# A new written-out order for all engines, and 26 small steps that change between ScalarE and VectorE

## The chip, the cores and the metric

The kernel runs on one core of a Trainium2 chip. A core has TensorE (matrix products into PSUM), VectorE and ScalarE (elementwise work; both read PSUM), GpSimd and SyncE (here almost only issuers of transfers). Each engine works through its own list of instructions in order and waits on semaphores for the others. The metric is the device time in microseconds of one execution. In the profile PE is TensorE's matmuls, PEld its weight loads, DVE VectorE, ACT ScalarE, POOL GpSimd, SP SyncE.

## What is computed

A block-sparse attention over 4 batches x 8 heads x 768 tokens x 64, followed by a gated feed-forward layer with a convolution of width 3 over the tokens:

```python
scores = scale * np.matmul(q, k.transpose(0, 1, 3, 2))
scores = np.where(mask, scores, -1000000000.0)      # window, first and last block, 3 sampled blocks a row
attn = np.exp(scores - max); attn = attn / (sum + 1e-09)
x = np.matmul(attn, v)                              # heads side by side: (4, 768, 512)
h = np.maximum(x @ w_in, 0.0)                       # 512 -> 1024
conv_out = sum of conv_w[k] * h shifted by k - 1    # along the tokens
out = (h * sigmoid(conv_out)) @ w_out               # 1024 -> 512
```

Inputs and output are float32; the kernel computes in bfloat16 with float32 sums.

## The kernel before

Heads go in pairs: `P` numbers the 16 pairs, four to a batch. For each pair, keys and queries are brought into a layout with the head's 64 columns and 24 mask rows on the partitions (tiles `e` and `o`, one of five slots), so that one product gives masked scores. For the first five pairs TensorE turns them (`k_tr`, line 470; `q_tr`, line 508) and ScalarE or VectorE copies the result (`k_cp`, `q_cp`; all copies go through `dcopy`, lines 328 for ScalarE and 330 for VectorE); for the others a transposing transfer on SyncE does (`xb`, line 585), and VectorE copies it to the slot (`stg_cp`). The mask rows are made once from small tiles (`nblk`, line 280, `a3`, `a4`, `m_q`, `m_k`) and copied to the other slots (`m_kc`, `m_kh`, `m_h1`, `m_slot`).

The attention is cut into 144 units of eight 128x128 blocks, in nine segments of tokens (two a batch, the last one split). Of each unit TensorE makes the scores in two halves (`s`, line 746, into one of two PSUM tiles `st`; the halves of unit u are s#2u and s#2u+1), ScalarE one exponential over 128x1024 (`exp`, line 757, to one of eight tiles `pt`), and TensorE the product with the values in two halves (`av`, line 779, into one of two tiles `av`). The values come by transfer and are copied by VectorE or ScalarE (`v_cp`, to `vt`). At the end of a pair VectorE divides by the sums (`rcp`, `norm`, lines 696 and 698) and the tokens are turned, by transfer (`x_xb`, line 707) or by TensorE (`x_tr`, line 717, with a copy `x_cp`).

The feed-forward part of a segment runs between the units of the next ones: `f1` (line 895) gives a feature chunk in one of two PSUM tiles `mix`; `relu` takes it out, on ScalarE (line 915) or VectorE (line 917); `mul` and `add` (lines 949, 959) are the convolution on VectorE, in the last segment `conv` (line 970) on TensorE; `tanh` (line 998 or 975) is ScalarE's; `g1`, `g2` (lines 1001, 1006) are the gate on VectorE; `f2` (line 825, at the very end line 810) is the output product, `ev` its eviction from PSUM on ScalarE or VectorE to `o2s`, and `out` the transfer to memory.

At the start TensorE runs 45 matmuls on a cleared tile (`warm`, line 1027; the tile is cleared by VectorE, `warm_mem`, line 224) and 12 more a little later (`fill`, line 1034).

The order of all this is not worked out when the program is built: the steps are collected in a graph, and `put_down` takes them in the order of a written-out text, `ORDER`. Two characters name a step; for a step that two engines can do a third names the engine (P, A, V, G, S); then come the numbers of the buffers that it takes. The order in the text is the order of each engine's list.

Of the kernel before, what the change touches and what calls it, by code (L numbers as in the profile page):

```python
# [25 lines left out]
1A0470S481O1490T4a1U44b1V4c2404d2634e271TV34f2c14g2e04h2f4i2k24j2m11aV1oV0N1pV5H65k5l5p5q5K15L5M75u5v5z5P05Q  # L26
5A05I4O15R05U15V5W15J5a05N610625O5S5T5X5Y6324PV00J5bV5B20D5C5Z35+661675D15EV6416b06c5/0651B160V0K1DV1CV6836d4
0w0v6g16hhq0hr6i56l06m6n6ht1hu6t16uhsV0hvVhO0hQhP6v7hI0hJ6y06zhw1hxhKA6A0hyVhRhS6D16E69hz0hA6F16a1P16e6f6j6I0
6k6J6ohBA1QVhW11RVhT6q0hX6r6K26Q1hF06RhGhC1hD6S3hEAhHVhU6V06W6+11W06p06/6X47056w6x6B73074hL1hM781756hNA796C6G
7a77g06H6L6M6T17h6U6Y1Z17i07l17m6Z717276777q07r7b7n1hYhZi221XV41YVi3i4h+hV06N1i5ia36O1+Vh/ib7d21/V25V4i0ic7ei6  # L30
7s27v17w7c0ii07jio17kid7D07E7x37o7p7t7u7y7z7F4i76s1280292g12h6P7f7I17J7N07G17H7O7A37K5i17P67Biei8i92aV02bVifig
ih2dV02iV17Cijip7S17Tiq7X07Lik7U77Y7M7Q7R831847Vir7Z0851880897Wil8d18e7+8a22jVisV04k2n4l2s34mimV18002lV12tV281
iu18i08j8f38k4ix0iyizV8q18riviwViS4iTiUiV8v08wiA0iBiD1iE8s58x6iCAiFAi+0iW2o22p2qV22rV2u2002v22x2w8A18B7/08F086
878GiG08b8c8g8hiJ1iH8C78H0iXiIA8l8m8t18K18L8S08T8uiK2108yj08n1i/8oj122ViLV23Vj61j28M18U28z8X18Y8D8E8I8J90091
8Z3925j38N8O08ViM1951iP0969769d08WiQiNiOA8+9e8/939i194989j998P2j7iYj8j4iZj98Qj59a3iRVja9bje29f79k1jfjgjhji9n0
9o9p3jE1jbjs09g19s19t9u69h9l9x09yjt9z79mjF9F19q9r9G9v9w9A9K09L9B0jcjdjGjujj9H19M62F2G42C2D02Q2I2H2N2O12R32T2S
2Y2Z22y08222z2J18p8R9c9P19Q9R4jkjljHjIV29C02AV39Djv9I9U09Va019Ja1jN1jOjwA39W0a22jK0jLjMA1jPV0Gk63a50a6aa1jQ19N
abjT0jRk7k8jSVk9jUa75ac3jVA2/30032312Kaf0agak1alah7jZ1j+am1j/A9O9SjW09T9X9Yas0a31ata4a8jXa9ax1ayk31k4ke4kakb0L
kg9Z10H2BVjYVkm0knkf2LV4au6az4aC0aDaE0k00adk1aH1aeaIk2AaiajanaP0aQaJ2jm0jnkh9+ki2MVap2k5Vkcku1aU1aVaR5aW3kjjo
aZ0a+jpao0avawb21b3jy1aAaBaFaGaKaLa/7aqkv2EV32PV4kpkd1kob70b8kqkxaM3kk2+V0aNkwkl9E32U22Vin330jxarit349/b46jqA4  # L40
jzbf1bgb94jAjBbk0kI0aS1blaTaXaYaObh0krbm2jCA1bp1b0bqb1b5kJbu0bvb6ksky2WV02XVktbr5kzkAkBkC1babb0kD373833a3b13f
3c3d3ebw13mbC1bDbc035V1kEkKbH0kFbE3bIbM1bNkLkGV339A1bdkMV036VkO1kPbibJ7bO6kQVbR0bSkR0kSbT4kTVla2lblcldlebW1bj
bXbnbobsbY0kX1c20c3btkU0c71c8c42c95kYkVbxbykWAkZVbz2bAli3cc0cdbF1bGch1cibKl11ce1lfbLl2cp0cj3cqk+0bPbQbUbVbZb+0
cu1ljlklll3Vlmb/1lgc0cr7lnlhloc5l71cvk/l0Alq4cz0c6cacbcfcgcAcw6l40lplrlsltl5l8ckcE1clcFcm3l9VlucB0l6Aly0lzcnlB
lAlC3p3n03q23u3r3s3tcG4cJ0cKcs1ctcxcycClM0cL2lvcR1lG1cDcScW0cT5cHcXcY3cIlNcMcN0lHcUcVc/1d0d40d5lDjDbe03g13hjJ
c1bB3v23wcokHd17lwlxd66cZlIc+lOdc1ddde43iV2lElFd2lP3jVlQV1lJdh0lKA2didj5dm1dnm20m3d3do73E3B3F43J3G3xV3m4V0cO0
cPme1mfmgV3yVdr0d7dsm50m6dw1d8dxdt1m7Vmq1mrmsmtmud913oV23H3T3U33C13Idy03Y3V3W3Q3R23X43443df1mb1dE0dFdG2m80m9mc
dJ1mdAmaAdadKdgdO0dPdL6dQ3mh1mk0mlmidkdT1dUdldpdqdudvmjAd/0e0dzmn1dV4e41e5dA0dHdImoe15e67mpAe90eaeb1mvmy2mmVmz
mG3mImHmJmKmAdB2mBdCmCmO4lS0dMdNdRee1dSefdWdXlTe21e3lY1eg0mLdY3mwmx0mPlUej0eklZl+lVe7l/mDmQdZmRmMmS3DV3mEel2
m0A3e8er1esecew0edehexet6kN3kjr3K03LlR3Z1cQ1lWA0mFn01eieB1eCemn1mN3MV4mTey3eD4mUmV3NVeo0epmW0mXen0mYmZeG0eH  # L50
m+A4n2n3db3+3/V03zlLdDn4V140V3SV4eO1eP3Pd+nf0m1423leq2lX3O3An5ngnc1nd45A0eI5eQ7neAnhVnC0eT0eUeY1eZn90nan61n7
eV1e+0nEnDnbVn8AnFnu1f10f2euevf61f7nl0ezf32nmni1fe0f86nvnGnwnHnxnnVffeAnjeEnkVfj1fkeFeJeKfg3fl4nynzeL1nK2nLeM
nMnIeR1eSeWeXfo0fpno0e/f0ft1fuf4f5fq5f9nr1nsfv7fa0fB0fCnpfhfG1fHfifmfnfrfsfwfxfb2nNnAnJnqVnBntAfcnOfy3nS3fD1
fI0fL0fMfzn+1fN2fT1fUfE1fFo40nTnUnVnWfY0fJfZfKnPfV641eNfdfAf+3nXnQfOn/o5nRg11g2fPfQ0fW0fXf/g90g0g34gao0o6gb5g4
ge1gffRnYnZo7o1o2V2o8A3gg7gj0gkg5om0ong610MooA1gl1op1oqgc1gr1g7orVoK4oMoLoNoOov0gsgt0os1gdowoxAgw0otouAgxgB1gh
# [1014 lines left out]
```

## Time and profile before

| | |
|---|---|
| runs | 204.57, 204.63, 204.76 us; median 204.63 |
| span of the profiled execution | 202.8 us |
| time around the span (median of the runs less the span) | 1.8 us, so the profiled execution's own time is about 204.6 |
| busy, of the span | PE 97%, ACT 94%, DVE 90%, POOL 28% |
| granted TensorE clock | full in all 40 slices |

The span goes from the first to the last instruction. A busy share is the sum of an engine's instructions without overlaps; as matmuls are pipelined and their ends are modelled, PE looks fuller than it is, and the distance from the start of one matmul to the start of the next says more than its length. In a timeline a row is: start, time from the first start to the last end, engine, line, operation, output<-input, shape, count, and in brackets the idle time before it with what ended it. In the chain a row is start, length, engine, output and line.

### The profile page before, as it was taken

The page shows a single profiled execution, that of the slowest core. Times are in us where ns is not written, and L with a number is a line of the kernel's source. Part 1 is how long each engine was busy: PE and PEld are TensorE (multiplying, and loading weights), DVE is VectorE, ACT ScalarE, POOL GpSimd, SP SyncE. Part 2 cuts the span into 40 slices and gives each one's busy share as a digit, 9 for nine tenths or more (in the row PEclk, how much of TensorE's full clock was granted, in tenths as well). Part 3 has the DMA queues.
Part 4 walks back from the last instruction along what each step waited for, and adds up shares of the span by engine and source line. Part 5 has one row for each costly group of instructions (what it writes and reads, how often), then busy time and mean ns, then how long its engine had stood idle before and what let it go on. Part 6 is the DMA issues. An engine that isn't in the chain of part 4 may idle for free.

```text
span 202.8 us, 6814 instructions
## 1 busy us (share of the span) xinstructions
PE 196.8 (97%) x2708; PEld 153.9 (76%) x2708; DVE 181.8 (90%) x572; ACT 189.7 (94%) x251; POOL 57.5 (28%) x112
## 2 busy tenths in 40 slices
PE   7899999999999999999999999999999999999993
PEld 7799977986788777877688877876678877876742
DVE  7999989999999979999899988999899968999950
ACT  6999999999999999999999998999999989998842
POOL 8870568630520354202534328400000000000000
PEclk9999999999999999999999999999999999999999
DMA  6999999999998399956869699994321202001515
GB/s 143 177 223 207 182 135 132 167 171 151 155 122 129 61 141 154 213 106 132 133 108 159 82 197 218 135 176 115 124 72 24 41 14 68 13 10 60 204 63 202
DMA packets 53655, 25.96 MB, mean 128 GB/s; under 512 B 39616, under 2 KB 50584, under 8 KB 53624
## 3 DMA queue, kind: packets, MB, share of 16 engines
q0 software_dynamic: 19984, 11.24, 43.7%
q1 hardware_dynamic: 33208, 13.87, 34.6%
q8 instruction: 21, 0.34, 0.7%
q10 hardware_dynamic: 432, 0.43, 0.6%
q14 instruction: 10, 0.08, 0.1%
HBM read 23.08 MB, written 6.29 MB: 145 GB/s over the span
## 4 chain that ended last, share of the span: by engine, by line
PE 78%; ACT 15%; issue 3%; DVE 2%; DMA 1%; ACTq 0%
PE st L746 25%; PE mix L895 18%; PE mix L825 17%; PE av L779 14%; ACT pt L757 11%; DMA o2s<-in_k_dram 1%; DVE e L330 1%; ACT m L998 1%; PE mix L810 1%; PE st L825 1%; PE av L970 1%; ACT nat L328 1%; PE mix L508 1%; ACT hE L915 0%; ACT o2s L328 0%
## 5 line engine op out<-in xcount | busy, mean ns | idle before, releaser
L757 ACT ACTIVATE pt<-st 128x1024 bf16<-128x1024 f32 x144 | 140.6, 1039 | 1.8 <-PE st L746 0.9
L779 PE MATMUL av<-vt,pt 128*128 128x65 bf16 x1152 | 59.9, 193 | 0.2 <-DVE vt L330 0.2
L779 PEld LDWEIGHTS <-pt 128*128 128x128 bf16 x1152 | 52.3, 97 | 9.9 <-issue 0.3
L895 PE MATMUL mix<-xT,winb 128*128 128x384 bf16 (+2 forms) x288 | 53.6, 308 | 0.1
L949 DVE TENSOR_SCALAR m<-hE,cw 128x382 bf16<-128x382 bf16 (+2 forms) x192 | 49.3, 316 | 0.5 <-ACT hE L915 0.2
L825 PE MATMUL mix<-woutb,gT 128*128 128x512 bf16 x176 | 47.1, 379 | 0.3 <-DVE gT L1006 0.3
L746 PE MATMUL st<-o 88*128 88x128 bf16 (+1 forms) x240 | 43.9, 229 | 0.4 <-ACT pt L757 0.3
L746 PE MATMUL st<-o,e 88*128 88x128 bf16 (+1 forms) x228 | 43.4, 233 | 0.0
L746 PE MATMUL st<-e,o 88*128 88x128 bf16 (+1 forms) x224 | 42.3, 234 | 0.2 <-ACT pt L757 0.2
L746 PE MATMUL st<-e 88*128 88x128 bf16 (+1 forms) x208 | 40.9, 239 | 0.1
L746 PEld LDWEIGHTS <-o 88*128 88x128 bf16 x464 | 34.7, 97 | 7.7 <-issue 0.8
L746 PEld LDWEIGHTS <-e 88*128 88x128 bf16 x436 | 33.0, 97 | 7.1 <-issue 0.4
L959 DVE TENSOR_TENSOR m<-m 128x764 bf16<-128x764 bf16 (+2 forms) x64 | 33.5, 532 | 0.4
L895 PEld LDWEIGHTS <-winb 128*128 128x128 bf16 x288 | 24.0, 97 | 8.0 <-issue 0.5
L998 ACT ACTIVATE m<-m 128x764 bf16<-128x764 bf16 (+2 forms) x32 | 26.3, 829 | 0.5 <-DVE m L959 0.3
L825 PEld LDWEIGHTS <-gT 128*128 128x128 bf16 x184 | 15.0, 97 | 9.3 <-DVE gT L1006 0.5
L417 POOL COPY pace<-pt 1x1 bf16<-1x1 bf16 x24 | 6.2, 257 | 49.9 <-ACT pt L757 49.8
L1006 DVE TENSOR_TENSOR gT<-m,hE 128x764 bf16<-128x764 bf16 (+3 forms) x36 | 18.0, 510 | 0.5
L698 DVE TENSOR_TENSOR xtok<-av,rcp 128x384 bf16<-128x384 f32 (+2 forms) x36 | 18.2, 506 | 0.3
L915 ACT ACTIVATE hE<-mix 128x384 bf16<-128x384 f32 (+2 forms) x36 | 17.7, 507 | 0.7 <-PE mix L895 0.5
L240 POOL DMA_DIRECT2D nat<-in_q_dram x23 | 16.8, 733 | 3.2 <-issue 2.5
L917 DVE TENSOR_SCALAR hE<-mix 128x384 bf16<-128x384 f32 x28 | 15.3, 549 | 2.6 <-PE mix L895 2.2
(84 smaller groups left out, 157.4 us busy)
## 6 DMA issues: line engine op xcount, KB each, us to landing
out_dram<-o2s SPq DMA_DIRECT2D x23, 256.0 KB
vn<-in_v_dram POOLq DMA_DIRECT2D x16, 192.0 KB, 5.0
nat<-in_k_dram POOLq DMA_DIRECT2D x15, 192.0 KB, 4.7
nat<-in_q_dram POOLq DMA_DIRECT2D x7, 192.0 KB, 5.2
winb<-in_moe_w_in_dram POOLq DMA_DIRECT2D x2, 512.0 KB, 9.5
woutb<-in_moe_w_out_dram POOLq DMA_DIRECT2D x4, 256.0 KB, 8.2
nat<-in_q_dram POOLq DMA_DIRECT2D x8, 96.0 KB, 4.5
nq<-in_q_dram POOLq DMA_DIRECT2D x5, 96.0 KB, 5.2
```

Of the source, the lines that this page charges most:

```text
L240: return op(name, {eng: occ}, lambda e: on(e).dma_start(out=dst(), in_=src), prio, deps, dma=(kind, service), **kw)
L698: nm = op("norm", {"DVE": t_dps(128 * C)}, lambda e: nc.vector.tensor_tensor(out=xtok_t[xk.index][:, 0:C].rearrange("p c h d -> p h c d"), ...
L746: nc.tensor.matmul(out=st[:, 128 * x:128 * (x + n_)], lhsT=QK[kc % 2][s][0:88, 1, hh, kc // 2, :], rhs=QK[par][s][0:88, 0, hh, idx:idx + n ...
L757: nc.scalar.activation(out=pt_t[ptb.index], in_=st_t[stb.index], func=AF.Exp, bias=0.0, scale=0.125)
L779: nc.tensor.matmul(out=o[:, off:off + 65], lhsT=pt_t[ptb.index][:, 128 * x:128 * x + 128], rhs=V_t[vslot_b[P].index][:, hh, kc, 0:65], sta ...
L825: nc.tensor.matmul(out=acc(), lhsT=gT_t[gb.index][:, ffc, 128 * t:128 * t + 128], rhs=woutb[:, ffc, :], start=(ffc == 0), stop=(ffc == NFF ...
L895: nc.tensor.matmul(out=mix_t[hb.index][:, w1 * y:w1 * y + w1], lhsT=winb[:, fc, 128 * ffc:128 * ffc + 128], rhs=xT_t[xt_buf[n].index][:, f ...
L915: i = nc.scalar.activation(out=dst, in_=src, func=AF.Relu, bias=0.0, scale=0.5)
L949: i = nc.vector.tensor_scalar(out=m_t[cb.index][:, x, y, 0:w], in0=hE_t[heb.index][:, f0 + y, t0 + x:t0 + x + w], scalar1=cw[:, x, f0 + y: ...
L959: nc.vector.tensor_tensor(out=m[:, a_, :, 0:w], in0=m[:, a_, :, 0:w], in1=m[:, b_, :, 0:w], op=ALU.add)
L998: th = [op("tanh", {"ACT": t_act(2 * w) + 0.04}, lambda e, cb=cb, w=w: nc.scalar.activation(out=m_t[cb.index][:, 0, :, 0:w], in_=m_t[cb.in ...
L1006: i = nc.vector.tensor_tensor(out=gT_t[gtb.index][:, f0:f0 + 2, t0:t1], in0=m_t[cb.index][:, 0, :, 0:w], in1=hE_t[heb.index][:, f0:f0 + 2, ...
```

## The change

Only the text `ORDER` is replaced. Both texts hold the same 1,789 steps. Every buffer number stays with the step that had it, and each buffer passes from user to user in the same sequence. The lists of SyncE and GpSimd, which issue nearly all transfers, are the same; the lists of TensorE, ScalarE and VectorE are in another order. 26 steps change their engine:

- from ScalarE to VectorE (16): `m_q#1`, `m_kh#1`, `m_h1#1` (mask rows), `q_cp#3`, `v_cp#11`, `v_cp#15`, `x_cp#6`, `relu#3`, `relu#21`, `relu#42`, `ev#2`, `ev#3`, `ev#4`, `ev#12`, `ev#21`, `ev#23`;
- from VectorE to ScalarE (10): `cast_k#1`, `k_cp#2`, `relu#20`, `relu#23`, `relu#25`, `relu#38`, `relu#44`, `ev#7`, `ev#13`, `ev#14`.

(A number counts the steps of a name as the code makes them.) The text itself, cut to its first and last lines:

```diff
--- before.py
+++ after.py
@@ -18,47 +18,47 @@
 ORDER = """
-000x010z020B0407080905060b1e00a1f1c01q11s11801m11t1E21G21H030y0e0c0gV0d0nV0f0A0i0hA0WA30UA0oAr41r5r6r7r8r9rarb
-rcrdrerfrgrhrirjrkrlrmrnrorprqrrrsrtrurvrwrx0Y01210ZA014A0VA13A0mA0XV0jV0+V0lV0t0uryrzrArBrCrDrErFrGrHrIrJrK
-15017A16ArLrM4n04o0/14s14t1g11j04p00q10V0p11V1hV11lV1kV4u11dV01iV4x04yrN0rOrPrQ4C14D4z2rRrSrTrUrVrWrXrY4H04I
-4E34J44q14r4v4w4Q14R4S54A4B4F4G0s0r1rV14V04W4K1u04X64+14/5071x11vV21yV1zV4L0530544T4U4Y4Z5c15d510E15505e10C1wV
-4M01FV24N0F0k5h05i1I0525j21JV35m15n5o31L1561NV575811MV5r05s5f15g5w15x1KV1911n00I5t45y55F05G1bV591S30O0P0Q0R46
...
-qr1qsqu1qvpQqCpRq60q7qDq0pXqtAqw3qG4qxq2q3qypYpZqc1qJ1qKqdqO0qL1qeqHq4qMq5q8q9qNqIqaA3qfqPqQqRqgA4qbqhqSA0qTS
-qU0qVqWqXq+1qYA2qZSq/r0r1r2Ar3A
+040708090500060WA30b1e00C0e0a0hV0c1f1c0021q1011s1180030d0UA1m10XA0gV1t1E21G21Hr41r50oVr6r7r8r9rarb0f0A0xrc0ird
+0Brerf0lVrgrhrirjrkrlrm0jVrnrorprq0Y0rr0nVrsrtrurvrw0ZA0121rx0t0mV13A0u0/1ryrzrArB14ArCrD10A4n00VA0+V4orErFrG
+rH11VrI4p0rJ150rKrLrM4s117V16A4t4x0rN0rO4u10q4y1g1rP0z1j00p0D4C11hV11lV4z24D0y4H01kVrQrR1dV01iV4IrS0r4q14r4E3
+4J44v4Q11rV14R4w1u04V04W4A4B4S54X64FrT4+14/1S34GrU1vV2rV1x1rW0s530rX1zV5071yV544KrY4L01FV20E14T1wV5c15d4U550
+5e14Y4Z514M00O5h05i521I00F5m14N5n1L1560P0Q570G1JV31NV5j21MV5r05s0R5f15o3191465t41KV1A05w15x5g5k5y5475l5F05G1bV
...
+pjolqFqtAq60qCqu1pXpRo3pYqvqc1q2q7pZqdqG4qHqw3qJ1qKqDq3qeq4qIofq5qL1q8qMq9qfqxqyqNqO0qPqgV4qQqaA3qRqSA0q+1q/
+qU0r0r1qVqbqhqWqXqYV2r2AqTSqZSr3A
 """
```

Read out, the lists of the three engines begin so. VectorE before:

```
ident_mem#0 v_one#0 warm_mem#0 v_one#2 a_mem#0 v_one#4 pad_mem#0 v_one#1 nblk#0 ident24#0 m_q#0 a3#0 m_h1#0
a4#0 v_one#3 m_k#0 cast_k#1 m_kc#0 k_cp#1 m_kh#0 m_slot#1 k_cp#2 m_slot#0 k_cp#3 k_cp#4 q_cp#7 q_cp#6 v_cp#0
k_cp#5 m_slot#3 m_slot#2 v_cp#1 k_cp#6 q_cp#10 q_cp#11 he_zero#0 k_cp#7 rcp#0 v_cp#2 norm#0
```

VectorE after:

```
ident_mem#0 he_zero#0 nblk#0 m_q#1 ident24#0 a_mem#0 warm_mem#0 pad_mem#0 a3#0 m_q#0 m_h1#1 a4#0 v_one#3
v_one#0 m_k#0 v_one#4 m_kh#0 m_kc#0 m_h1#0 m_kh#1 k_cp#1 k_cp#3 q_cp#3 m_slot#1 v_one#2 m_slot#0 he_zero#1
k_cp#4 q_cp#7 v_one#1 q_cp#6 v_cp#0 k_cp#5 m_slot#2 v_cp#1 k_cp#6 m_slot#3 q_cp#11 q_cp#10 v_cp#2
```

ScalarE before, then after (`ld_` are transfers that it issues):

```
ld_q0#0 ld_k0#1 m_q#1 cast_k#0 cast_q#0 m_h1#1 k_cp#0 q_cp#1 cast_q#1 q_cp#0 m_kh#1 q_cp#3 q_cp#2 exp#0 exp#1
exp#2 exp#3
...
ld_q0#0 ld_k0#1 cast_k#0 cast_q#0 cast_k#1 k_cp#0 q_cp#0 q_cp#1 k_cp#2 cast_q#1 exp#0 q_cp#2 exp#1 exp#2 exp#3
exp#4 exp#5
```

TensorE before, then after:

```
warm x30 k_tr#0 q_tr#0 warm x13 q_tr#1 warm x2 s#0 s#1 k_tr#1 s#2 s#3 k_tr#2 q_tr#3 s#4 s#5 fill x4 s#6 s#7
fill x8 s#8 s#9 av#0 av#1 av#2 av#3 s#10 s#11 av#4 av#5 av#6 av#7
...
warm x23 k_tr#0 warm x6 q_tr#0 warm x1 k_tr#1 warm x6 s#0 s#1 warm x6 q_tr#1 warm x3 s#2 s#3 s#4 fill x2 s#5
k_tr#2 fill x1 q_tr#3 s#6 s#7 s#8 fill x2 s#9 fill x1 av#0 av#1 av#2 s#10 s#11 av#3 k_tr#3 s#12 s#13 av#4 av#5
av#6 fill x1 s#14 s#15 av#7
```

Further on: VectorE has `v_cp#14`, `ev#12`, `stg_cp#20` and `stg_cp#21` ahead of `norm#24` where it had them (the eviction: ScalarE) behind it, and `relu#42` follows `norm#24`; TensorE has `f1#80` and `f1#81` ahead of `f1#82`, `f1#83`, `s#238` and `s#239`, not behind them. In the last steps TensorE ends with the first column half of the last block, not the second; the evictions `ev#21` and `ev#23` are VectorE's, `ev#20`, `ev#22` and `ev#24` stay ScalarE's.

More of the change, by code (lines that the diff above doesn't have):

```diff
@@ L26 @@
[L26 to L55, printed above, removed]
```

38 lines of the change are left out of this document (34 added, 4 removed).

## The prediction

> **What bounds the kernel now.** I read the page's busy shares and its chain first, then the chain in order of time, then the PE's own timeline for the places where it really stands still.
>
> ```profile
> span 202.8 us, 6814 instructions
> PE 196.8 (97%) x2708; PEld 153.9 (76%) x2708; DVE 181.8 (90%) x572; ACT 189.7 (94%) x251; POOL 57.5 (28%) x112
> PE 78%; ACT 15%; issue 3%; DVE 2%; DMA 1%; ACTq 0%
> ```
>
> The chain of work that ended last lies on TensorE for 78% of the span. Busy shares overstate (ends of matmuls are modelled), so I look at starts in the chain:
>
> ```profile
> 39.13 0.94 ACT pt L757
> 40.11 0.87 ACT pt L757
> ...
> 84.08 0.44 PE st L746 x6
> 84.53 0.33 PE mix L895 x2
> 84.85 0.12 PE av L779 x4
> ```
>
> Around 40 us exponentials follow each other; at 84 us a piece of TensorE work starts when the one before it ends (84.08 + 0.44 = 84.52, 84.53 + 0.33 = 84.86). That holds from 67 to 189 us. So the end is set by three things: when TensorE begins real work, how much work it has (unchanged here), and where it stands still. Once the head is past, the larger standstills are these (TensorE's timeline; a row whose next row starts late hides a gap):
>
> ```profile
> 18.51 0.41 PE L779 MATMUL av<-vt,pt 128*128 128x65 bf16 x8
> 18.98 0.22 PE L746 MATMUL st<-o 88*128 88x128 bf16 x1
> ...
> 41.81 0.28 PE L779 MATMUL av<-vt,pt 128*128 128x65 bf16 x4
> 42.10 0.22 PE L746 MATMUL st<-o 88*128 88x128 bf16 x1
> ...
> 47.59 0.27 PE L746 MATMUL st<-e,o 88*128 88x256 bf16 x1
> 48.14 0.61 PE L825 MATMUL mix<-woutb,gT 128*128 128x512 bf16 x2 [0.28 <-DVE gT L1006]
> ...
> 66.43 0.28 PE L779 MATMUL av<-vt,pt 128*128 128x65 bf16 x4
> 66.99 0.22 PE L746 MATMUL st<-o 88*128 88x128 bf16 x1 [0.28 <-ACT pt L757]
> ...
> 189.01 1.58 PE L895 MATMUL mix<-xT,winb 128*128 128x128 bf16 x20
> ```
>
> Four av matmuls take 0.12 us (the 84.85 row), so the gaps are 0.47 - 0.24 = 0.23, 0.29 - 0.12 = 0.17, 0.55 - 0.11 = 0.44 and 0.56 - 0.12 = 0.44; the 20 short matmuls at 189 would take 19 x 0.056 + 0.22 = 1.28, so 0.30 is waiting. Together **1.58 us**. That is what a better order can win behind the head, and the whole size of the question.
>
> **The change, part by part.** *Buffers and transfers.* Every buffer index stays with its user, and the lists of SyncE and GpSimd are the same. Cost 0 by themselves; a transfer moves only as far as its producer does.
>
> *The head, TensorE's start.* Rows of VectorE and TensorE before:
>
> ```profile
> 0.82 0.11 DVE L223 MEMSET ident<- 128x64 uint32 x1 [0.82 <-PEq L1054]
> ...
> 0.94 0.11 DVE L224 MEMSET warm<- 128x64 uint32 x1
> ...
> 1.36 0.53 DVE L280 COPY nblk<-ident 24x768 bf16<-24x768 bf16 x1
> ...
> 1.82 0.40 DVE L267 CAST ident<-ident 24x24 f32<-24x24 bf16 x1
> 2.22 0.47 DVE L300 TENSOR_SCALAR e<-nblk 24x256 bf16<-24x256 bf16 x2
> ```
>
> ```profile
> 1.10 3.22 PE L1027 MATMUL st<-warm 128*128 128x128 bf16 x30 [1.10 <-DVE warm L224]
> 4.20 0.34 PE L470 MATMUL mix<-ident,nat 128*128 128x128 bf16 x3
> ...
> 4.79 0.90 PE L1027 MATMUL st<-warm 128*128 128x128 bf16 x13
> ```
>
> The memset of the warm-up tile was VectorE's third instruction. In the new list it stands behind nblk, which cannot start before 1.36 because it reads GpSimd's identity, one pair of mask rows (0.47, taken over from ScalarE), the small cast (0.40) and another memset (0.1). So it starts near 1.36 + 0.46 + 0.47 + 0.40 + 0.1 = 2.8 to 2.9 and the first warm-up 0.16 later (0.94 to 1.10): **3.05 instead of 1.10**. TensorE takes its list in order, and 23 warm-ups stand ahead of the first key transposes. Thirty took 4.20 - 1.10 = 3.10 us, 0.104 each while the clock is still slow (later thirteen took (0.90 - 0.22)/12 = 0.057 each), so 23 take 2.4 and the key transposes start at about **5.45 instead of 4.20**. ScalarE's share:
>
> ```profile
> 4.96 0.47 ACT L328 COPY e<-mix 64x384 bf16<-64x384 bf16 x1
> 5.45 0.26 ACT L328 COPY o<-mix 64x128 bf16<-64x128 bf16 x1
> 5.74 0.35 ACT L328 CAST nat<-o2s 128x192 bf16<-128x192 f32 x1
> 6.12 0.37 ACT L328 COPY e<-mix 64x256 bf16<-64x256 bf16 x1
> ...
> 7.58 4.66 ACT L757 ACTIVATE pt<-st 128x1024 bf16<-128x1024 f32 x5
> ```
>
> Three slow transposes need 0.5 until the last is out, so the key copy starts near 6.0 (was 4.96); with 0.47, 0.37 and 0.26 behind it the last query copy ends at 7.1, and the first scores start at 7.2; before they followed the copy that ended at 6.12 + 0.37 = 6.49. Loss there 0.7. Ahead of the first exponential ScalarE now has another key copy (taken from VectorE, costed as the 0.47 row) and the cast of head 1 (0.35): it starts near 8.0, against 7.58.
>
> *The head, VectorE.* Head 1's query transposes need that cast, so they run at 8.1. Their second copy was ScalarE's and is now VectorE's, ahead of the mask copies to slot 1; behind it VectorE's whole list waits until about 8.35.
>
> ```profile
> 7.05 0.70 DVE L330 COPY o<-o 24x1536 bf16<-24x1536 bf16 x1
> ...
> 8.15 0.76 DVE L330 COPY e<-e 24x1536 bf16<-24x1536 bf16 x1
> ...
> 9.32 0.55 DVE L330 COPY e<-mix 64x768 bf16<-64x768 bf16 x1
> ...
> 10.65 0.57 DVE L330 COPY vt<-vn 128x768 bf16<-128x768 bf16 x1
> ```
>
> ```profile
> 11.28 0.64 PE L779 MATMUL av<-vt,pt 128*128 128x65 bf16 x16 [0.21 <-DVE vt L330]
> ```
>
> 8.35 + 0.3 for the copy, + 0.72 + 0.78 for the two mask copies (starts to next starts) gives 10.15. The key copy of pair 1 (was 9.32) also waits for its transposes, which TensorE now does behind the scores of unit 2: 10.4. From there to the value copy was 10.65 - 9.32 = 1.33, and that copy takes 0.57: it ends at 12.3, and the first av, which before too waited for it, starts at **12.35 instead of 11.28**, 1.07 later. Six filler matmuls (0.057 each) and one av step (0.12), which stood ahead of unit 5's scores in the gaps, now stand behind them, where TensorE has no gap: 0.46. TensorE is then late by 1.0 to 1.5 when unit 10's scores start; **I take +1.4**. Bounds: 0.7 (only the first scores' loss, the rest absorbed) and 1.5.
>
> *The Trainium skill, beside this.* The rows show the full rate about 3 us after the first warm-up. The Trainium skill (TensorE: Matmul & The Clock Gate, Part 1) says that the clock opens after about 3.4 us of sustained activity, counted in a window that runs freely. By that the full rate would come at 6.45 or later instead of 6.0, and up to eight more warm-ups and transposes of the head would run at half rate. This is the third rival below.
>
> *The middle.* ScalarE loses the relu at 32.5 us ahead of the standstills of 41 to 67 us, and has one 0.37 copy more behind its first exponential; so its load against TensorE there is as before, and as TensorE arrives 1.4 late but ScalarE only about 1, part of the 0.23 + 0.17 + 0.44 + 0.44 goes. Bounds 0 and -1.58 (with the one at 189); **I take -0.9**. The exchanges of relus and evictions from 67 us on cost nothing while TensorE stays the later one; ScalarE's idle is their cover.
>
> *140 to 165 us, VectorE.* Rows of VectorE before:
>
> ```profile
> 143.49 0.56 DVE L698 TENSOR_TENSOR xtok<-av,rcp 128x384 bf16<-128x384 f32 x1
> ...
> 145.01 0.69 DVE L330 COPY o2s<-mix 128x512 f32<-128x512 f32 x1 [0.50 <-PE mix L825]
> 145.73 0.56 DVE L330 COPY o<-stg 64x1536 bf16<-64x1536 bf16 x1
> 146.32 0.36 DVE L330 COPY vt<-vn 128x768 bf16<-128x768 bf16 x1
> ```
>
> The normalisation at 143.49 gets two slot copies (0.56 each), a value copy (0.36) and an eviction taken from ScalarE (costed as the 0.69 row) ahead of it: 2.2 us. Behind it waits a relu taken from ScalarE, and for its bank wait feature matmuls that TensorE has moved 1.1 us closer. Bounds 0 and +2.2; I take +0.3, the size of TensorE's existing wait for VectorE (0.28 at 48.14).
>
> *The tail.* The last eviction moves to VectorE:
>
> ```profile
> 199.59 0.37 ACT L328 COPY o2s<-mix 128x256 f32<-128x256 f32 x1 [0.50 <-PE mix L810]
> ```
>
> At the ratio of the 145.01 row to the same copy on ScalarE it costs below 0.1 more; its transfer goes out through SyncE instead of ScalarE. I take 0, bounds -0.1 and +0.1.
>
> **Sum.** +1.4 - 0.9 + 0.3 = **+0.8** on a span of 202.8, so 203.6. The median of the runs, 204.63, is 1.8 above the span; the forecast is 204.63 + 0.8 = **205.4**.
>
> **Rivals.** *Faster: the standstills of 18 to 67 and 189 us all go.* TensorE arrives late, so ScalarE gets ahead and every exponential is ready. For it: ScalarE's list is the shorter one later on. Against: it must win over 1.4 + 0.4 to be told from no change, and 1.58 is all there is, unless the head loses only its lower bound. With 0.7 - 1.58 = -0.9 it gives 203.7. It decides where the head's loss stays under 1.1. *No change:* the head's loss and the gains cancel within 0.4. *VectorE becomes the bound at 140 to 165 us:* 1.4 - 0.9 + 2.2 = +2.7, 207.3. For it: VectorE is 90% busy, takes on five evictions of 512 columns and gives back three. Against: it stood idle 0.50 at 145.01. *The clock opens late:* eight instructions at 0.104 instead of 0.057 are 0.4 more in the head: 205.8.
>
> **How the numbers follow.** About 0.2% (0.4 us) is what can be told from no change. Forecast 0.45; late clock 0.07; VectorE 0.13: slower 0.65. No change 0.17. Faster 0.18. The range runs from the fast rival, 203.7, to VectorE's bound, 207.3; past each end lies less than a tenth.
>
> **What would show it.** In the changed profile: first warm-up near 3.05, first key transposes near 5.45, first exponential near 8.0, first av near 12.35 behind a wait for VectorE's vt; standstills of 41 to 67 us smaller; TensorE without gaps from 67 to 140; waits for VectorE near 146 to 165. I am wrong if the first av starts before 11.8, or if waits over 1 us appear on TensorE elsewhere.

## The result and the profile after

The changed kernel takes **215.04 us** (median of four runs, 212.10 to 216.47), the kernel before beside it on the same chip 204.60 (204.49 to 204.76). The ratio is **1.0454, 95% interval 1.0384 to 1.0524**: slower by about 9.3 us (0.0454 x 204.6). Ratios are worked out from the fast runs alone, which leaves out the one of 216.47, so they are not the quotients of the medians. The forecast was 205.4 with a range of 203.7 to 207.3: the sign was right, the size far out of the range.

The profiled run is the fastest of the four, 212.10 us with a span of 210.3. Page of the changed kernel (busy times, chain, two groups of instructions):

```profile
span 210.3 us, 6827 instructions
PE 200.1 (95%) x2708; PEld 155.3 (74%) x2708; DVE 183.3 (87%) x579; ACT 187.9 (89%) x244; POOL 59.0 (28%) x112
PE 51%; DVE 32%; DMA 8%; ACT 3%; issue 3%; POOL 0%; DVEq 0%; POOLq 0%
L757 ACT ACTIVATE pt<-st 128x1024 bf16<-128x1024 f32 x144 | 141.6, 1038 | 6.8 <-PE st L746 6.0
L895 PE MATMUL mix<-xT,winb 128*128 128x384 bf16 (+2 forms) x288 | 56.9, 312 | 3.0 <-DMA xT<-xtok 2.4
```

The chain, which lay on TensorE for 78%, lies there for 51% now; VectorE has 32% and the DMAs 8%. (VectorE's share is not all its own: at 146.43, below, the chain goes from a transpose back to a gate step of VectorE that the transpose does not read.) ScalarE's exponentials wait 6.0 us for scores, and the feature matmuls 2.4 us for a transfer, in one piece.

To see where the time goes, compare the starts of the same exponential in both traces (their order is the same). At these times of the kernel before, the changed one is late by:

| start before, us | 8 | 15 | 30 | 50 | 58 | 68 | 88 | 127 | 138 | 149 | 159 | 170 |
|---|---|---|---|---|---|---|---|---|---|---|---|---|
| late by, us | 1.0 | 1.4 | 1.7 | 1.2 | 1.5 | 2.2 | 2.7 | 2.9 | 3.2 | 7.1 | 7.4 | 6.8 |

Three parts: 1.4 us in the head, a slow growth to 3.2, and a step of 3.9 between 138 and 149 us. The last is the largest and has a plain cause. (This is the fastest of four executions; the part between 26 and 73 us is larger in the traces of runs 1 and 2 below.)

**The step at 138 to 149 us.** One step of VectorE was moved by 114 us: `m_l#0`, three small scalings that make `mlast`, the mask for the last tile (line 344). VectorE's timeline, before and after:

```profile
16.75 0.46 DVE L344 TENSOR_SCALAR mlast<-nblk 24x128 bf16<-24x128 bf16 x3
```

```profile
130.48 0.69 DVE L344 TENSOR_SCALAR mlast<-nblk 24x128 bf16<-24x128 bf16 x3
```

Its first reader is a transfer, `m_last#0` (`o<-mlast`, line 240), and that stands in the list of SyncE, which issues in order. SyncE's waits after, then its timeline before and after:

```profile
SPq L240 <- DVE mlast L344: 9.3, 1, 9.3
```

```profile
118.09 1.05 SPq L833 DMA_DIRECT2D out_dram<-o2s  x2
119.25 0.90 SPq L240 DMA_DIRECT2D o<-mlast  x1
...
137.44 1.23 SPq L707 DMA_TRANSPOSE xT<-xtok  x1
...
139.69 1.20 SPq L707 DMA_TRANSPOSE xT<-xtok  x1
```

```profile
120.45 1.07 SPq L833 DMA_DIRECT2D out_dram<-o2s  x2
130.86 0.90 SPq L240 DMA_DIRECT2D o<-mlast  x1
...
144.18 1.23 SPq L707 DMA_TRANSPOSE xT<-xtok  x1
...
146.43 1.20 SPq L707 DMA_TRANSPOSE xT<-xtok  x1
```

SyncE stands 9.3 us in front of a small mask transfer. Behind it wait transposes that have nothing to do with the mask: block transposes into `stg`, then the transposes of the attention output into `xT`, which leave 6.7 us late (144.18 and 146.43 for 137.44 and 139.69). They do not wait for their own producers. The step that feeds the first of the two, `norm#22`, is even 1.9 us earlier than before (VectorE, before and after), and still its transpose leaves 11 us behind it:

```profile
134.44 0.55 DVE L698 TENSOR_TENSOR xtok<-av,rcp 128x384 bf16<-128x384 f32 x1
```

```profile
132.57 0.55 DVE L698 TENSOR_TENSOR xtok<-av,rcp 128x384 bf16<-128x384 f32 x1
```

Not all of the 9.3 us is new: in the kernel before SyncE stood at 122 us for a load (its waits from 118 to 131 us):

```profile
SPq L585 <- DMA nat<-in_q_dram: 5.4, 1, 5.4
```

TensorE needs the last of the late transposes. Chain of the changed kernel, TensorE's timeline, and the windows (busy of PE, PEld, DVE, ACT, POOL, then granted clock, DMA share, GB/s):

```profile
146.43 4.80 DMA xT<-xtok
```

```profile
148.20 0.65 PE L895 MATMUL mix<-xT,winb 128*128 128x384 bf16 x3
151.27 1.52 PE L895 MATMUL mix<-xT,winb 128*128 128x384 bf16 x5 [2.42 <-DMA xT<-xtok]
...
152.70 0.42 PE L746 MATMUL st<-e,o 88*128 88x256 bf16 x1
152.91 0.31 PE L746 MATMUL st<-o 88*128 88x128 bf16 x1
...
155.07 0.27 PE L746 MATMUL st<-e 88*128 88x256 bf16 x1
155.18 0.22 PE L746 MATMUL st<-o,e 88*128 88x128 bf16 x1
```

```profile
140.00:150.00 10.00, 8.56 (x77) 5.14 (x75) 9.42 (x27) 9.07 (x12) 0.00 (x0) 1.00 0.49 110
150.00:160.00 10.00, 8.73 (x94) 6.36 (x94) 6.70 (x21) 5.86 (x8) 0.00 (x0) 0.83 0.29 93
```

TensorE stands for 2.42 us, and then it runs at half rate: a matmul of 256 columns takes 152.91 - 152.70 = 0.21 us, and 0.11 again from 155.07. A granted clock of 0.83 over 10 us is some 1.7 us of lost work more. 2.4 + 1.7 = 4.1, about the size of the step.

**The head.** TensorE, ScalarE and VectorE after:

```profile
2.73 2.63 PE L1027 MATMUL st<-warm 128*128 128x128 bf16 x23 [2.73 <-DVE warm L224]
5.16 0.52 PE L470 MATMUL mix<-ident,nat 128*128 128x128 bf16 x3
...
7.65 0.42 PE L746 MATMUL st<-e 88*128 88x256 bf16 x1
7.86 0.31 PE L746 MATMUL st<-o,e 88*128 88x128 bf16 x1
...
8.25 0.27 PE L746 MATMUL st<-e 88*128 88x256 bf16 x1
8.36 0.50 PE L1027 MATMUL st<-warm 128*128 128x128 bf16 x6
...
12.69 0.49 PE L779 MATMUL av<-vt,pt 128*128 128x65 bf16 x11
```

```profile
8.56 1.02 ACT L757 ACTIVATE pt<-st 128x1024 bf16<-128x1024 f32 x1 [0.44 <-PE st L746]
```

```profile
9.01 0.23 DVE L330 COPY o<-av 64x128 bf16<-64x128 bf16 x1 [0.75 <-PE av L508]
```

The head went the way the prediction told, step by step: late warm-ups, late key transposes, VectorE held up by the query copy that it took over (the 0.75 us at 9.01), and the first av 1.41 us later (12.69 for 11.28).

### The profile page after: what moved, and what is told of

The parts are those of the page before. It is cut to its first block, busy times and chain, and to the rows that moved or that the text cites. A ratio compares the mean times of both kernels' runs of the same rounds, so it can differ in the third digit from the quotient of the medians.

```text
span 210.3 us, 6827 instructions
## 1 busy us (share of the span) xinstructions
PE 200.1 (95%) x2708; PEld 155.3 (74%) x2708; DVE 183.3 (87%) x579; ACT 187.9 (89%) x244; POOL 59.0 (28%) x112
## 4 chain that ended last, share of the span: by engine, by line
PE 51%; DVE 32%; DMA 8%; ACT 3%; issue 3%; POOL 0%; DVEq 0%; POOLq 0%
PE st L746 14%; PE mix L825 12%; PE mix L895 10%; DVE m L949 10%; PE av L779 8%; DVE m L959 6%; DVE hE L917 3%; DMA stg<-nat 3%; ACT pt L757 3%; DVE xtok L698 3%; DVE gT L1006 2%; DVE e L330 2%; DMA xT<-xtok 2%; DMA nat<-in_q_dram 2%; PE st L1027 2%
## 5 line engine op out<-in xcount | busy, mean ns | idle before, releaser
L779 PE MATMUL av<-vt,pt 128*128 128x65 bf16 x1152 | 64.9, 193 | 0.2 <-DVE xtok L698 0.2
L779 PEld LDWEIGHTS <-pt 128*128 128x128 bf16 x1152 | 55.1, 97 | 11.7 <-ACT pt L757 1.2
L895 PE MATMUL mix<-xT,winb 128*128 128x384 bf16 (+2 forms) x288 | 56.9, 312 | 3.0 <-DMA xT<-xtok 2.4
L746 PE MATMUL st<-o 88*128 88x128 bf16 (+1 forms) x240 | 45.9, 230 | 0.2 <-ACT pt L757 0.2
L746 PE MATMUL st<-o,e 88*128 88x128 bf16 (+1 forms) x228 | 44.9, 234 | 0.0
L746 PE MATMUL st<-e,o 88*128 88x128 bf16 (+1 forms) x224 | 44.2, 235 | 0.1
L746 PE MATMUL st<-e 88*128 88x128 bf16 (+1 forms) x208 | 42.0, 240 | 0.3 <-ACT pt L757 0.2
L917 DVE TENSOR_SCALAR hE<-mix 128x384 bf16<-128x384 f32 x26 | 14.1, 551 | 9.3 <-PE mix L895 7.2
L915 ACT ACTIVATE hE<-mix 128x384 bf16<-128x384 f32 (+2 forms) x38 | 18.9, 511 | 1.4 <-PE mix L895 1.2
L240 POOL DMA_DIRECT2D nat<-in_q_dram x23 | 18.5, 805 | 3.2 <-issue 2.9
```

The lines of the kernel that those rows point to most:

```text
L746: nc.tensor.matmul(out=st[:, 128 * x:128 * (x + n_)], lhsT=QK[kc % 2][s][0:88, 1, hh, kc // 2, :], rhs=QK[par][s][0:88, 0, hh, idx:idx + n ...
L779: nc.tensor.matmul(out=o[:, off:off + 65], lhsT=pt_t[ptb.index][:, 128 * x:128 * x + 128], rhs=V_t[vslot_b[P].index][:, hh, kc, 0:65], sta ...
L895: nc.tensor.matmul(out=mix_t[hb.index][:, w1 * y:w1 * y + w1], lhsT=winb[:, fc, 128 * ffc:128 * ffc + 128], rhs=xT_t[xt_buf[n].index][:, f ...
L915: i = nc.scalar.activation(out=dst, in_=src, func=AF.Relu, bias=0.0, scale=0.5)
L917: i = nc.vector.tensor_scalar(out=dst, in0=src, scalar1=0.5, scalar2=0.0, op0=ALU.mult, op1=ALU.max)
```

## The experiments

Every kernel computes the whole reference. Step names as in the lists of steps: `norm` scales an attention output (VectorE, line 698), `x_xb` is SyncE's transpose of it into `xT` (line 707), `xb` SyncE's transpose of a loaded block into `stg` (line 585), `stg_cp` VectorE's copy out of `stg` (line 330). The runs came from several chips, on which the kernel before took 204.88 to 205.89 us in the median and single runs of it 204.06 to 208.17; so each is given as a ratio to the kernel before on its own chip. Medians are of 4 to 12 executions.

| what runs | median, us | before | ratio (95% interval) |
|---|---|---|---|
| 1 after, mask early | 211.08 | 205.28 | 1.0260 (1.0204 to 1.0316) |
| 2 as 1, warm-up tile early | 210.47 | 205.28 | 1.0249 (1.0215 to 1.0282) |
| 3 before, mask late | 206.41 | 205.28 | 1.0064 (1.0037 to 1.0090) |
| 4 before, warm-up tile late | 205.89 | 205.28 | 1.0036 (1.0003 to 1.0070) |
| 5 as 2, six copies late | 211.37 | 204.94 | 1.0309 (1.0248 to 1.0371) |
| 6 order of before to 26 us | 213.54 | 204.94 | 1.0288 (1.0206 to 1.0369) |
| 7 order of before to 73 us | 206.84 | 204.94 | 1.0076 (1.0044 to 1.0107) |
| 8 order of before to 142 us | 205.72 | 204.94 | 1.0028 (0.9995 to 1.0061) |
| 9 before, norm#4 late | 206.88 | 205.22 | 1.0079 (1.0039 to 1.0119) |
| 10 as 2, way to x_xb#0 early | 210.88 | 205.22 | 1.0208 (1.0085 to 1.0331) |
| 11 before, three steps late | 209.01 | 205.22 | 1.0165 (1.0083 to 1.0247) |
| 12 before, exchanges of engine alone | 219.19 | 205.89 | 1.0672 (1.0617 to 1.0728) |
| 13 as 10, engines of before | 214.37 | 205.89 | 1.0428 (1.0371 to 1.0485) |
| 14 order of before to 49 us | 209.31 | 205.89 | 1.0159 (1.0070 to 1.0248) |
| 15 as 14, norm#11 early | 207.91 | 204.88 | 1.0140 (1.0092 to 1.0189) |
| 16 before, norm#11 late, stg_cp#8 early | 206.49 | 204.88 | 1.0061 (1.0025 to 1.0097) |

### The mask of the last tile (1 and 3)

```diff
 # VectorE's list, changed kernel (run 1)
 cw#0
+m_l#0
 norm#0
...
 mul#49
-m_l#0
 stg_cp#17
```

> The changed kernel with one VectorE step moved: the three small copies to mlast stand early again (behind cw#0, as before), not near 130 us. Theory A (a blocked transfer queue): SyncE's list stands still for 9 to 10 us behind the one transfer that reads mlast, so token transposes arrive late at 144 to 151 us and TensorE waits. Then SyncE's wait for mlast is gone, the transposes that were issued at 144.2 and 146.4 us come near 139 to 142, the wait of 2.4 us for xT goes, TensorE keeps its full clock, and the time falls by 4 to 6 us to 206.5 to 209, with runs within 1 us of each other. Theory B (VectorE's load at 140 to 165 us, as my prediction had it for its last rival): the normalisations stay late and the time stays at 211 to 215.

```diff
 # VectorE's list, kernel before (run 3)
 cw#0
-m_l#0
 k_cp#8
...
 mul#49
+m_l#0
 mul#50
```

> The kernel before with that one VectorE step alone moved late (behind the same convolution multiply, mul#49, as in the changed kernel; near 128 us there). Theory A: SyncE stands still from 119 to about 128 us, time 208.5 to 211, and TensorE waits for xT near 140 to 150 us. Theory B: the time stays at 204.4 to 205, since the transfers behind it have 10 us in hand.

Putting one step of 0.69 us back brings the ratio from 1.0454 to 1.0260, with intervals that do not touch: 1.9% of the time, or about 4 us, the size of the step in the trace. The time that theory A gave, 206.5 to 209, did not come: 211.08 is at the lower end of what B had, because about 5 us are lost elsewhere. The trace of run 1 tells the two apart. SyncE does not wait for `mlast`, TensorE has no wait for `xT`, and the exponentials are as late at 149 us as at 146 (6.8 us; in the changed kernel 3.1 and 7.1). But they are 4.7 us late at 66 us already and 6.9 at 88, so that the profiled run ends at 211.77 us, hardly below the 212.10 of the changed kernel, and its transposes leave at 145.88 and 148.15, not near 139 to 142. It is the slowest of its four executions, and the other was the fastest of its four; the gain shows in the ratio and in this one step.

In the kernel before the same slip costs much less, 1.0064 or 1.3 us, between the two expectations. Run 3, SyncE's and TensorE's timelines:

```profile
128.31 0.90 SPq L240 DMA_DIRECT2D o<-mlast  x1
```

```profile
147.57 0.97 PE L895 MATMUL mix<-xT,winb 128*128 128x384 bf16 x5 [0.52 <-DMA xT<-xtok]
```

SyncE is blocked there too (9.1 us later than 119.25), but the transposes leave only 4 us late, TensorE stands for 0.52 us and keeps its full rate. So the price of a blocked queue is not that of the block: it is what remains when the slack behind it is used up. In the changed kernel the last of these transposes left 2.7 us later than in run 3 (146.43 for 143.69) and took 4.8 us to land instead of 3.8, while TensorE came to need it only 1.8 us later; 2.7 + 1.0 - 1.8 is the 1.9 us by which its wait is longer. The half rate came on top.

### The warm-up tile (2 and 4)

```diff
 # VectorE's list, changed kernel (run 2, beside the edit of run 1)
 ident_mem#0
+warm_mem#0
 he_zero#0
...
 a_mem#0
-warm_mem#0
 pad_mem#0
```

> As the run before it, and the memset of the warm-up tile is VectorE's second instruction again (behind the identity's). Theory A (the late warm-up delays TensorE's start and its full clock): first warm-up near 1.0 to 1.1 us, key transposes near 4.2, first exponential 0.5 to 1.0 earlier, time 0.6 to 1.4 us below the run before it. Theory B (the head is lost on ScalarE's and VectorE's lists): the first av stays within 0.3 us of 12.7 and the time within 0.3 us.

```diff
 # VectorE's list, kernel before (run 4)
 v_one#0
-warm_mem#0
 v_one#2
...
 m_q#0
+warm_mem#0
 a3#0
```

> The kernel before with the memset of the warm-up tile alone moved behind nblk, the small cast and the first mask rows: first warm-up near 2.7 us and, with thirty of them ahead, key transposes near 5.9 instead of 4.2. Theory A: TensorE's work behind has too few gaps to take it up, time 205.3 to 206.6. Theory B: the standstills up to 67 us absorb it, time 204.4 to 204.9.

In the order of before the late tile costs 1.0036, some 0.7 us, as theory A had it; in the profiled run the exponentials are 1.4 us late up to 41 us and 1.2 from 50 us to the end, a shift that hardly changes. In the changed order, giving it back is worth only 1.0260 to 1.0249 (0.6 us between the medians, the least that theory A gave), which the intervals do not tell from nothing.

### Copies, and where in the order the rest is lost (5 to 8)

With mask and warm-up tile repaired, some 5 us were still open. Run 2's VectorE waits for transposed blocks, and TensorE behind it:

```profile
59.42 0.55 DVE L330 COPY e<-stg 64x1536 bf16<-64x1536 bf16 x1 [2.51 <-DMA stg<-nat]
```

```profile
66.72 0.48 PE L895 MATMUL mix<-xT,winb 128*128 128x384 bf16 x2 [1.84 <-DVE hE L917]
```

The copy stands earlier in VectorE's list than it did before. Run 5 puts six such copies back behind the steps that they followed:

```diff
 # VectorE's list, run 2 -> run 5 (the first two of six)
 relu#8
-stg_cp#4
 mul#12
-stg_cp#5
...
 add#9
+stg_cp#4
+stg_cp#5
 add#10
```

> As the run with the mlast copies and the warm-up memset early (210.5 us), and six slot copies of VectorE (stg_cp 4, 5, 7, 8, 10, 11), which read transposing transfers, go back behind the convolution steps that they followed before. Theory A (VectorE's list waits for a transfer that is not there yet, with relus behind it that TensorE waits for): VectorE's wait for stg near 58 us (1.8 us and more) goes, TensorE's wait for a relu near 65 us goes, and the time falls by 2 to 3.5 us to 207 to 208.5. Theory B (the loss there is TensorE's own order): the time stays at 210 to 211.

1.0309: no gain, against theory A. TensorE's timeline of run 5:

```profile
61.83 0.28 PE L746 MATMUL st<-e 88*128 88x256 bf16 x1 [1.10 <-DVE e L330]
62.86 0.22 PE L746 MATMUL st<-o,e 88*128 88x128 bf16 x1 [0.75 <-DVE o L330]
```

The blocks are no earlier, and TensorE stands for the copies instead of for the features. So the early copies alone are not the cause; the transposes are late. (In run 2 the block for the copy at 59.42 left SyncE at 53.31; in the kernel before at 50.53.)

Runs 6 to 8 (and 14 below) take the list of all steps of before up to one exponential and the changed list from there, with mask and warm-up tile early throughout:

```diff
 # the list of all steps
-changed[0:n]
+before[0:n]            # n = 308 (exp#20, 26 us), 694 (exp#60, 73 us), 1316 (exp#115, 142 us)
 the other steps as changed
```

> The order before up to the exponential of unit 20 (near 26 us), mlast copies and warm-up included, and from there the changed order. Against the run with both early (210.5 us) it shows what the rest of the head costs. Theory A (q_cp#3 ahead of the slot masks on VectorE delays the first av): TensorE is less than 0.3 us late at 25 us, and the time falls by 0.8 to 1.5 us, to 209 to 209.7. Theory B (later waits take the head's loss up): within 0.4 us of 210.5.

> The order before up to the exponential of unit 60 (near 73 us), then the changed order. Theory A (one place, 57 to 67 us, costs 2.5 us or more beside the head): 205.5 to 207. Theory B (the changed order loses a little everywhere): 207.5 to 209.

> The order before up to the exponential of unit 115 (near 142 us), then the changed order, which has most of its last evictions and gate steps in another place. Theory A: the tail itself costs within 0.6 us either way: 204.5 to 206. Theory B, a tail that wins what the new order was to win: below 204.

The old head does not help (1.0288 with the cut at 26 us, 1.0249 without it): what it saves is lost again behind the cut. From 26 to 73 us on the ratio falls to 1.0076, and to 1.0028 at 142 us, which can hardly be told from 1. Run 6 met neither expectation, runs 7 and 8 met their theory A. So most of what remains is lost by the order between 26 and 73 us, and nearly nothing by that of the last 60 us, once the mask is early. In the trace of run 2 the loss shows as two steps: 1.2 us late at 58 us and 4.1 at 66, 3.9 at 81 and 5.3 at 88.

A warning came with run 8. Up to 142 us its order is that of before, yet its profiled run loses 1.9 us at 50 to 58 us. VectorE:

```profile
52.45 0.78 DVE L330 COPY e<-stg 64x1536 bf16<-64x1536 bf16 x1 [2.10 <-DMA stg<-nat]
```

The kernel before stands close to an edge there: in its own profile the same copy starts at 50.47, and its block landed at 50.38 (by the trace's semaphore events); in run 8 the block landed at 52.36, 10.7 us behind its issue instead of 9.3. A single profile with such a step proves nothing about an edit; only the medians do.

### What starts SyncE's burst: norm#4 (9 to 11)

From `x_xb#0` on (35.13 us in the kernel before), SyncE issues transposes for 17 us with gaps of 0.1 us; then it stands 3.5 us for a load, and again at 61 us. So the expectation below, back to back to 72 us, overstates: there is some room. `x_xb#0` waits for `norm#4`, which the changed order has some 3 us later.

```diff
 # VectorE's list, kernel before (run 9)
 mul#4
-norm#4
 relu#5
...
 k_cp#11
+norm#4
 mul#7
```

> The kernel before, with one step of VectorE moved: norm#4 stands behind k_cp#11 instead of behind mul#4, some 3.2 us later, as in the changed kernel. It feeds x_xb#0, the transfer behind which SyncE's list holds every transpose of the next 35 us (x_xb#0 was issued at 35.13 us in the kernel before, at 38.36 in the changed one). Theory C (the burst of transposes has no room to catch up: SyncE issues it back to back from x_xb#0 to 72 us): x_xb#0 at 38.2 to 38.5, the copies stg_cp#2 to #5 wait for their transposes, TensorE is 1.5 to 2.5 us late at 70 us and stays so: 206.5 to 207.5 us beside 205. Theory D (the transposes have room, and what the changed kernel loses between 26 and 72 us comes from the order of VectorE and TensorE themselves): VectorE waits under 1 us more, 205.0 to 205.6 us.

SyncE's and TensorE's timelines of run 9:

```profile
38.66 1.52 SPq L707 DMA_TRANSPOSE xT<-xtok  x1
```

```profile
55.85 0.32 PE L895 MATMUL mix<-xT,winb 128*128 128x384 bf16 x1 [1.82 <-DMA xT<-xtok]
```

206.88 us, ratio 1.0079: one step moved by 3 us costs 1.6 us. The time is the one expected of a burst without room, but the wait is not where it was expected: no copy out of `stg` stands (the wait for the load fell from 3.5 to 1.3 us and took part of the slip up), TensorE stands 1.82 us for `xT` itself. The late step of this run and the one in run 8 are at the same place, so the profile alone would not do; the interval excludes no change.

```diff
 # run 2 -> run 10: TensorE's list, then VectorE's
 q_tr#8
-s#53
-s#54
 av#40
...
 av#43
+av#44
+s#53
+s#54
 s#55
 f1#10
-av#44
...
 relu#3
+rcp#4
+norm#4
 mul#3
...
-rcp#4
 add#2
-norm#4
```

> The changed kernel with the mask of the last tile and the warm-up tile early (the run of 1.0249), and with the way to x_xb#0 shortened: av#40 to av#44 ahead of s#53 on TensorE, rcp#4 and norm#4 directly behind relu#3 on VectorE. Theory C: x_xb#0 goes out at about 35.5 to 36 us instead of 37.9, VectorE's wait for stg (2.5 us at 59 us) falls to under 1 us, and 1.5 to 2.5 us come back: 208 to 209 us, ratio 1.013 to 1.019. Theory D: x_xb#0 is early all the same, but the ratio stays at 1.022 to 1.028 (210 to 211 us).

`x_xb#0` left at 36.44 us (37.92 in run 2), and the ratio is 1.0208 with an interval of 1.0085 to 1.0331: between both expectations, and not told from run 2. VectorE's wait at the copy fell from 2.51 to 0.49 us, as theory C had it, but the time did not follow: TensorE stands 1.39 us at 89.47 for a relu (0.45 us in run 2 at 88.53). Undoing the slip in the changed order did not bring back what making it costs in the old one.

```diff
 # VectorE's list, kernel before (run 11): the edits of runs 3, 4 and 9 together
-warm_mem#0, norm#4, m_l#0 at their places
+warm_mem#0 behind m_q#0, norm#4 behind k_cp#11, m_l#0 behind mul#49
```

> The kernel before with the three slips together: the warm-up tile set behind the query masks, norm#4 behind k_cp#11, and the mask of the last tile behind mul#49. Each step keeps its engine, and nothing else moves. If these three explain the changed kernel (theory C with the blocked lists), 210 to 214 us, ratio above 1.025. If the rest of the new order is needed as well (theory D), the sum of single prices: +1.3 for the mask, +0.8 to 1.2 for the warm-up, and 0 to 0.6 for norm#4: 206.5 to 208, ratio 1.008 to 1.015.

1.0165: between the two expectations. The single ratios of runs 3, 4 and 9 add up to 1.0179, so in the order of before the three prices add, as far as the intervals tell, to 3.4 to 3.7 us, where the whole change costs 9.3. They don't explain the whole change.

### Exchanges of engine, places in the order (12, 13)

```diff
 # run 12: the list of before, 26 steps on the engine of the changed kernel
-m_q#1 ScalarE, cast_k#1 VectorE, relu#3 ScalarE, ... ev#23 ScalarE
+m_q#1 VectorE, cast_k#1 ScalarE, relu#3 VectorE, ... ev#23 VectorE
 # run 13: the opposite, in the list of run 10
```

> The kernel before with the 26 exchanges between ScalarE and VectorE alone: the list of all steps, and so the place of every step among the others, is that of before. Theory E (the exchanges carry what is left of the loss): 208 to 210 us, ratio above 1.015, with VectorE waiting or late at 26 to 36 us (relu#3) and at 80 to 150 us. Theory F (the new places of the steps carry it): 205 to 206.3 us, ratio under 1.006.

> The changed kernel with the three slips repaired (the run of 1.0208), and the 26 steps given back to the engines that they have in the kernel before; the places of all steps stay those of the changed kernel. Theory E: 205.5 to 207.5 us, ratio 1.002 to 1.011. Theory F: it stays at 209.5 to 212 us, ratio 1.018 to 1.03, since the places are those of the changed kernel.

Both theories fell. Exchanges in the old places: 1.0672, worse than the whole change and far above the 208 to 210 us of theory E. Old engines in the new places: 1.0428, where the same list with the new engines has 1.0208. Each set of engines goes with its own order, and the two halves of the change can't be priced apart this way: an exchanged step lands in its new engine's list wherever the text of the other order happens to have it.

### A second late producer: norm#11 (14 to 16)

> The order of before up to the softmax step exp#40 (some 49 us), and from there the changed order, with the exchanges that lie there; the mask of the last tile stays early. The same cut gave 1.0288 at exp#20 (26 us) and 1.0076 at exp#60 (73 us). Theory G (what is left is lost in one place, the late start of SyncE's burst at 35 us and its neighbours): 206.5 to 207.5, as with the cut at exp#60. Theory H (the loss is spread over the stretch in proportion to its length): half of the way between the two, 208.5 to 211 us.

The cut at 49 us (n = 506) gives 1.0159, between the cuts at 26 us (1.0288) and at 73 us (1.0076), as theory H had it. That speaks for a loss that is spread, but the interval, 1.0070 to 1.0248, does not exclude one place. In its profiled run one step is clear, VectorE's and TensorE's timelines:

```profile
84.55 0.55 DVE L330 COPY e<-stg 64x1536 bf16<-64x1536 bf16 x1 [1.77 <-DMA stg<-nat]
```

```profile
87.24 0.49 PE L895 MATMUL mix<-xT,winb 128*128 128x384 bf16 x2 [1.76 <-DVE hE L917]
```

The expectation was that the block's transpose `xb#9` was late because it stood in SyncE's list behind `x_xb#7`, and that waited for `norm#11`, 3.3 us later than before (71.5 for 68.2), while the copy stood earlier in VectorE's list. Run 15 moves `norm#11`; run 16 makes the same squeeze in the kernel before.

```diff
 # VectorE's list, run 14 -> run 15
 relu#15
+rcp#11
+norm#11
 mul#21
...
 mul#23
-rcp#11
 mul#22
 add#14
-norm#11
 add#15
```

> The run with the cut at exp#40, with rcp#11 and norm#11 moved forward to directly behind relu#15 on VectorE, nothing else. In that run norm#11 came at 71.5 us (68.2 in the kernel before), x_xb#7 behind it at 72.09, xb#9 behind that in SyncE's list at 76.41, so that stg_cp#8 stood 1.77 us at 84.55 and TensorE 1.76 at 87.24 behind relu#21. Theory I (a late producer for SyncE's list and an early consumer squeeze the transposes' time): x_xb#7 at about 70, xb#9 at 74.5, the two waits fall under 0.4 us, and 1.4 to 1.8 us come back: 207.5 to 208, ratio 1.008 to 1.012. Theory J (the waits only pass on the lateness of VectorE, which is behind for its own reasons): x_xb#7 moves, but the time stays at 1.014 to 1.018.

VectorE's timeline of run 15, the same copy:

```profile
83.21 0.54 DVE L330 COPY e<-stg 64x1536 bf16<-64x1536 bf16 x1
```

`x_xb#7` left at 70.39 instead of 72.09, the copy does not stand, and TensorE's standstill at 87 us is gone. The profiled run ends 2.9 us earlier (207.67 for 210.53). The medians are 1.4 us apart, but on two chips, and the ratios 1.0159 and 1.0140 have intervals that overlap: the time is that of theory I, the ratio that of J.

The trace does not bear out the way that theory I told. `xb#9` left at 75.67, only 0.7 us earlier than in run 14 (76.41), not at 74.5. Behind `x_xb#7` SyncE stood for the block's load in both, first run 14, then run 15:

```profile
SPq L585 <- DMA nat<-in_q_dram: 3.1, 1, 3.1
```

```profile
SPq L585 <- DMA nat<-in_q_dram: 4.0, 1, 4.0
```

So the load set when `xb#9` left, not `norm#11`; it stood for that load in the kernel before too (3.5 us) and left at 73.57. GpSimd issued the load at 72.19 us in run 14, at 71.93 in run 15, at 69.79 in the kernel before. And the transpose took 8.1 us to land in run 14 (84.53), 5.4 in run 15 (81.02) and 4.9 in the kernel before (78.43, by the trace's semaphore events). With 5.4 us the block of run 14 would have been there at 81.8 us, a microsecond ahead of the copy. Whether the place of `norm#11` had a part in the slow landing, these runs do not show.

```diff
 # VectorE's list, kernel before (run 16)
 add#13
-norm#11
 mul#21
...
 g1#6
+norm#11
 g2#6
...
 mul#29
+stg_cp#8
 rcp#13
...
 mul#28
-stg_cp#8
 add#18
```

> The kernel before with two steps of VectorE moved, as they lie in the changed kernel: norm#11 behind g1#6 (about 3 us later) and stg_cp#8 behind mul#29 (about 3 us earlier). Theory I: x_xb#7 at 71.5 to 72, xb#9 at 76 to 76.5, VectorE waits 2 to 2.5 us for stg at 82 us, and 1 to 2 us of it reach TensorE through relu#20: 206 to 207.3, ratio 1.005 to 1.010. Theory J: VectorE waits, but the TensorE has other work meanwhile, and the time stays within 0.3 per cent of before.

```profile
77.85 0.97 PE L895 MATMUL mix<-xT,winb 128*128 128x384 bf16 x5 [0.80 <-DMA xT<-xtok]
```

206.49 us, 1.0061: the time expected, again by another wait than expected. `xb#9` left at 74.50, not at 76 to 76.5, and the copy did not stand; TensorE stood 0.80 us for the `xT` that `norm#11` feeds (TensorE's row above), and every later exponential is 1.0 us later than those ahead of it. What the trace shows is the price of a late `norm#11` through its own transfer; of the earlier copy it shows none.

## Why the prediction was wrong

**The step that failed** is the first of its parts, "Buffers and transfers": "the lists of SyncE and GpSimd are the same. Cost 0 by themselves; a transfer moves only as far as its producer does." The lists are the same, but the 0 does not follow, and the last clause is false: the transpose fed by `norm#22` left 6.7 us later although its producer was 1.9 us earlier. The producers of the transfers ahead of it were not followed. `m_l#0` moved by 114 us; its transfer could not leave at 119.25 any more, and in a list that goes in order everything behind it waited as well. TensorE's 2.42 us and the half rate after it, which come of that, are about 4 of the 9.3 us (run 1; in the order of before the same slip costs 1.3, run 3). `norm#4` and `norm#11` are the same failure in a smaller size: 1.6 us (run 9) and, with `stg_cp#8`, 1.3 us (run 16) when done in the order of before. The mask alone does not account for the miss: with it put back (run 1) the time is still 211.08 us, outside the range, and the second step that failed is "the middle" below.

**The head, +1.4**: right by mechanism and by size within the trace. First warm-up 2.73 (forecast 3.05), key transposes 5.16 (5.45), first exponential 8.56 (8.0), VectorE's wait till 9.01 (8.35), first av 12.69 (12.35), the exponentials 1.4 late at 15 us. Part of it was the rival of the late clock: at 7.65 the first score matmul takes 0.21 us, half rate, 4.9 us after the first warm-up; 0.11 is first seen between 8.25 and 8.36. The Trainium skill (TensorE: Matmul & The Clock Gate, Part 1) has about 3.4 us of sustained work in a window that runs freely; here it took 5.5 us (8.25 - 2.73). That rival's 205.8 did not come because of the rest. As a price, the late warm-up tile alone is +0.7 us in the median (run 4).

**The middle, -0.9**: the sign was wrong. In the profiled execution the exponentials go from 1.4 us late at 15 us to 3.2 at 138, in run 2 from 0.7 to 5.8. The argument was that a late TensorE would find ScalarE ahead, with bounds 0 and -1.58 that left no room for a loss; but 1.58, the sum of the standstills of before, bounds what can be won, not what can be lost. New waits came: in the repaired orders for transposed blocks (2.51 us at 59 us in run 2). Runs 6, 14 and 7 place most of it in the order between 26 and 73 us. With mask and warm-up tile repaired some 5 us are left (run 2).

**140 to 165 us, VectorE, +0.3**: a standstill came in this stretch, at 151.27, but for a transfer, not for VectorE. In run 1, without that wait, VectorE is busy for 24.6 of the 25 us from 140 to 165, and yet the exponentials are hardly later at 166 us than at 139 (7.5 and 7.4 us): VectorE as the bound was not the rival that won.

**The tail, 0**: run 8, in which only the last 60 us are in the new order, is at 1.0028 (0.9995 to 1.0061). No price of that stretch can be told from nothing.

**The condition for being wrong**, "waits over 1 us appear on TensorE elsewhere", is met by the row at 151.27. The mechanism that cost most, an in-order list of transfers blocked by a late producer, was not among the rivals named.

**What stays open.** With mask, warm-up tile and `norm#4` repaired, the changed order is still at 1.0208 (run 10), about 4 us. The cuts put it in the order between 26 and 73 us. In the traces of runs 1, 2, 6 and 10 it shows at the same two copies out of `stg`, near 60 and 86 us, each time with TensorE behind (1.8, 1.8, 1.9 and 0.7 us at 67; 1.4, 0.5, 1.1 and 1.4 at 88 to 90). Why the blocks land too late for them stays open: `norm#4` has a part at the first, by run 9's price, but repairing it did not bring the time back (run 10); at the second the block waited for its load and landed slowly (run 14). No run was faster than the kernel before.
